# The second w2 block's remainder moved behind the last product group, and four terms of the first down tile moved into the second tile

## The chip, the cores and the metric

The kernel runs on one core of one Trainium2 chip. What is compared is the device time of one execution in microseconds (us). The kernel before took 725.92 us (median of 3 runs, 725.57 to 726.45). One more execution was taken with the hardware profiler on, and it is that one that all the rows below come from.

The engines are named as in the profile: PE is TensorE (matmul), PEld its weight load, DVE is VectorE, ACT is ScalarE, POOL is GpSimd, SP is SyncE, which issues most transfers.

## The reference

Attention with a decay over 8 batches and 8 heads, then a mixture of 8 experts that routes every one of the 4608 rows to one expert:

```python
def _moe_ref(x, w_gate, w1, w2):
    N, D, E, F = (4608, 512, 8, 1024)
    ...
    for e in range(E):
        mask = expert_idx == e
        ...
        xe = x[mask]
        h = np.maximum(xe @ w1[e], 0.0)
        ye = h @ w2[e]
        out[mask] = gate_w[mask, None] * ye
    return out.astype(np.float32)
```

All inputs and outputs are float32.

## The kernel before

The first half of the time is attention; the change does not touch it. From about 364 us on the kernel works through the experts 1 to 7 in one pattern, and every engine's instructions stand in an order that is written out by hand: the code runs through steps, and lists of tasks say which helper is called after which step.

**Two-part numbers.** A float32 product is made of three matmuls. Each operand is kept as a rounded part and a remainder (operand less rounded part), and a term is rounded times rounded, rounded times remainder, or remainder times rounded. For a weight block ACT makes the rounded part (a CAST) and DVE or POOL makes the remainder (a TENSOR_TENSOR subtraction, whose two inputs and whose output all lie in SBUF).

**Up phase of an expert** (`sevens`, L1515): h = relu(x @ w1), made by a scheme with seven products per group of columns, in four product groups 0 to 3, each of 7 x 6 matmuls: 168 in all, of 320, 288 or 256 columns depending on how many rows the expert has. After some of the products a step of `group` runs: ACT and DVE take the banks apart, and the last steps of a group (`end` and `last`: L1561 on ACT, L1592 and L1564 on DVE) write h as its rounded part `hh` and its remainder `hl`. For group 3 these last steps come after the last matmul of the phase, at the head of the down phase. DVE's steps there are, in order, L1581, L1582, L1583, L1564, L1592 and three more L1564.

**Down phase** (`down`, L1277): y = h @ w2 for five tiles m = 0 to 4 of 128 rows, each with 24 terms of 512 columns, 8 values of ft with 3 terms each. w2 comes in four blocks of two ft: block 1 is ft 2 and 3, block 3 is ft 6 and 7. `round_v(e, i)` is the CAST of block i on ACT (L1458), `rest_v(i)` its remainder on DVE (L1451), `split_v` is both. In the trace the remainders' tiles are called w_1w for all blocks; in the instruction order they are w2_0_1w (blocks 0 and 1) and w2_1_1w (blocks 2 and 3), while w2_0_0w and w2_1_0w are the rounded parts.

In tile 0 the values of ft come in the order 0, 1, 2, 4, 5, 6, 3, 7, since h of ft 3 and 7 is written last, and the terms that use block 3's remainder, (6, 0, 1) and (7, 0, 1), are put off: `finish_down` makes them after the first quarter (6 terms) of tile 1.

**The order around the change.** In the up phase the tasks hang on products 0 to 27. For experts 2 to 7, block 0 is split after product 10, block 2 after 16, block 1 after 23 (CAST and remainder), and block 3 gets its CAST after 24; its remainder is put off to the head of the down phase, behind the last steps of group 3:

```python
for i, k in enumerate((15, 22, 16) if e == 1 else (10, 23, 16)):
    at(ups, (k, S(self.split_v, i)))
at(ups, (23 if e == 1 else 24, S(self.round_v, 3)))
...
dns.setdefault(0, [])[:0] = [*self.ends, T(self.rest_v, 3)]
```

Behind that remainder DVE goes on with transposes of the next expert's rows (`flip`, L1180). POOL meanwhile works for the next expert: two sets of four additions (`sums_s`, L1398 to L1401, 128x256, all in SBUF), then two remainders of w1 (`rest_s`, L1419, 128x1024 and 128x768), which need a CAST of ACT (L1413) that stands behind the last L1561; then the scatters of finished rows (L1308). A tile's result leaves its bank through ACT (L1305); tiles 0, 2 and 4 use one bank, 1 and 3 another, and the next up phase's product 3 (T4) uses tile 4's bank.

## Time and profile before

| | us |
|---|---|
| median of 3 runs | 725.92 |
| the profiled execution's own time | 724.27 |
| its span, first to last instruction | 722.5 |
| PE busy in the span | 714.3 (99%) |
| DVE, ACT, POOL busy | 564.9, 498.6, 570.7 |
| mean granted TensorE clock | 0.994 |

The profiled execution is 1.65 us under the median, and 1.8 us of it lie outside the span. Rows of the timeline read: start in us from the span's start, duration in us, engine, line, operation, output tile <- input tiles, shapes, count of instructions put together, and in brackets the idle time of the engine before it with what ended it.

### The profile page before, as it was taken

The page shows a single profiled execution, that of the slowest core. Times are in us where ns is not written, and L with a number is a line of the kernel's source. Part 1 is how long each engine was busy: PE and PEld are TensorE (multiplying, and loading weights), DVE is VectorE, ACT ScalarE, POOL GpSimd, SP SyncE. Part 2 cuts the span into 40 slices and gives each one's busy share as a digit, 9 for nine tenths or more (in the row PEclk, how much of TensorE's full clock was granted, in tenths as well). Part 3 has the DMA queues.
Part 4 walks back from the last instruction along what each step waited for, and adds up shares of the span by engine and source line. Part 5 has one row for each costly group of instructions (what it writes and reads, how often), then busy time and mean ns, then how long its engine had stood idle before and what let it go on. Part 6 is the DMA issues. An engine that isn't in the chain of part 4 may idle for free. (4 is left out here: it accounts for less than half of the span.)

```text
span 722.5 us, 18439 instructions
## 1 busy us (share of the span) xinstructions
PE 714.3 (99%) x6321; PEld 617.4 (85%) x6321; DVE 564.9 (78%) x1610; ACT 498.6 (69%) x1319; POOL 570.7 (79%) x701
## 2 busy tenths in 40 slices
PE   9999999999999999999999999999999999999997
PEld 4788888888888888898999898898898898988985
DVE  6667888888888888771879859879589799897730
ACT  6999999999999999662646555566465575655631
POOL 6999989898989898884589779688788797997411
PEclk9999999999999999999999999999999999999999
DMA  7775787777777667244348376286475584673300
GB/s 197 197 195 165 195 215 192 212 191 209 204 203 197 216 193 231 81 165 129 111 163 271 118 233 206 96 265 195 149 220 165 175 240 136 217 216 116 119 30 35
DMA packets 98724, 127.59 MB, mean 177 GB/s; under 512 B 10287, under 2 KB 56367, under 8 KB 98608
## 3 DMA queue, kind: packets, MB, share of 16 engines
q1 hardware_dynamic: 91568, 106.12, 50.5%
q0 software_dynamic: 6400, 19.93, 8.6%
q8 instruction: 71, 1.16, 0.6%
q14 instruction: 45, 0.37, 0.2%
q10 hardware_dynamic: 640, 0.01, 0.0%
HBM read 99.12 MB, written 27.93 MB: 176 GB/s over the span
## 5 line engine op out<-in xcount | busy, mean ns | idle before, releaser
L422 ACT ACTIVATE sc<-sc,nmx 128x512 f32<-128x512 f32 (+3 forms) x256 | 142.3, 558 | 5.4 <-DVE nmx L379 4.3
L1515 PE MATMUL ps<-X_0w,w1s 128*128 128x320 f32 (+2 forms) x504 | 107.0, 303 | 0.2 <-DVE u L1574 0.2
L1277 PE MATMUL ps<-w_0w,hl 128*128 128x512 f32 x272 | 107.2, 394 | 0.0
L1277 PE MATMUL ps<-w_0w,hhw 128*128 128x512 f32 x273 | 106.3, 390 | 0.0
L1277 PE MATMUL ps<-w_1w,hhw 128*128 128x512 f32 x272 | 105.5, 392 | 0.0
L1308 POOL DMA_INDIRECT out<-y,si_fast x40 | 47.4, 1186 | 70.0 <-ACT y L1305 39.5
L467 ACT COPY aT<-ps 128x512 f32<-128x512 f32 (+1 forms) x224 | 93.4, 506 | 1.6 <-PE ps L455 0.5
L330 POOL TENSOR_TENSOR hl<-raw,hl 128x640 fp32r<-128x640 f32 (+1 forms) x60 | 89.6, 1494 | 5.0
L526 PE MATMUL ps<-aT,va_t 128*64 128x256 f32 (+3 forms) x896 | 91.2, 355 | 0.0
L1515 PEld LDWEIGHTS ps<-X_0w,w1s 128*128 128x128 f32 x504 | 82.3, 188 | 0.7 <-DVE u L1574 0.5
L526 PEld LDWEIGHTS ps<-aT,va_t 128*64 128x64 f32 x896 | 56.9, 138 | 28.9 <-issue 5.4
L403 PE MATMUL ps<-hl 64*128 64x512 f32 (+1 forms) x720 | 80.4, 340 | 0.0
L1515 PE MATMUL ps<-X_1w,w1s 128*128 128x320 f32 (+2 forms) x252 | 75.9, 301 | 0.0
L379 DVE CUSTOM_DVE_ANT_0 sc<-ps,bias 128x128 f32<-128x128 f32 (+1 forms) x128 | 59.8, 486 | 9.7 <-PE ps L403 4.6
L1305 ACT ACTIVATE y<-ps,g_fast 128x512 f32<-128x512 f32 x40 | 27.9, 698 | 56.5 <-PE ps L1277 52.6
L1419 POOL TENSOR_TENSOR w1s<-w1r,w1s 128x768 fp32r<-128x768 f32 (+1 forms) x32 | 62.7, 1968 | 0.1
L1277 PEld LDWEIGHTS ps<-w_0w,hhw 128*128 128x128 f32 x273 | 51.2, 188 | 11.4 <-ACT hhw L1561 0.3
L1277 PEld LDWEIGHTS ps<-w_1w,hhw 128*128 128x128 f32 x272 | 51.1, 188 | 11.6
L1277 PEld LDWEIGHTS ps<-w_0w,hl 128*128 128x128 f32 x272 | 51.1, 188 | 10.9 <-DVE hl L1564 0.5
L379 DVE CUSTOM_DVE_ANT_1 sc<-ps,bias 128x256 f32<-128x256 f32 (+1 forms) x128 | 57.7, 488 | 2.9 <-PE ps L403 2.8
L1515 PE MATMUL ps<-xa,w1s 128*128 128x320 f32 (+2 forms) x336 | 56.0, 302 | 0.3 <-PEq L1289 0.3
L403 PEld LDWEIGHTS ps<-hl 64*128 64x128 f32 x720 | 52.3, 185 | 3.3
(246 smaller groups left out, 1899.5 us busy)
## 6 DMA issues: line engine op xcount, KB each, us to landing
bias<-ud SPq DMA_DIRECT2D x30, 576.0 KB, 5.8
w1r<-in_w SPq DMA_DIRECT2D x112, 128.0 KB, 2.6
w<-in_w SPq DMA_DIRECT2D x28, 512.0 KB, 6.6
raw<-in_qkT SPq DMA_DIRECT2D x64, 160.0 KB, 3.5
raw<-in_qkT SPq DMA_DIRECT2D x64, 144.0 KB, 3.7
va_t<-in_va SPq DMA_DIRECT2D x32, 256.0 KB, 5.8
x_dram<-row SPq DMA_DIRECT2D x32, 256.0 KB, 2.3
xs<-xg SPq DMA_DIRECT2D x30, 256.0 KB, 3.5
```

Source lines behind the costliest of these rows:

```text
L330: return eng.tensor_tensor(hl[:, 1], raws[n][:, r : r + w], hl[:, 0].bitcast(F32), ALU.subtract)
L379: red_last[:] = [V.tensor_tensor_reduce(dst, src, in1, -0.125, init, ALU.add, ALU.min, nms[n][:, col : col + 1]).ins]
L403: note(nc.tensor.matmul(pb[j][:, o : o + w], q[js], k[js], start=(i == 0), stop=(i == len(terms) - 1),))
L422: A.activation(x, x, AF.Exp, bias=nms[n][:, 5 * j + t : 5 * j + t + 1], scale=-1.0, accum_out=ssums[b][:, t, 2 * p + j : 2 * p + j + 1])
L467: copy_on = {"a": lambda o, i: A.copy(o, i), "v": lambda o, i: V.tensor_copy(o, i)}
L526: note(nc.tensor.matmul(pv[j * HD : (j + 1) * HD, q0 - qa : qb - qa], l, r, start=(blk == 0), stop=(blk == nb - 1),))
L1277: c.note(nc.tensor.matmul(py, rows(hi_, ft), self.w2p[e, ft][wi], start=k == 0, stop=k == len(terms) - 1, skip_group_check=tail or head,))
L1305: nc.scalar.activation(y, py, AF.Copy, scale=g[:, s : s + 1])
L1308: nc.gpsimd.indirect_dma_start(out=self.out, out_offset=bass.IndirectOffsetOnAxis(ap=si[:, s : s + 1], axis=0), in_=y, in_offset=None, bou ...
L1419: (eng or self.nc.vector).tensor_tensor(lo, raw, hi.bitcast(F32), ALU.subtract)
L1515: self.nc.tensor.matmul(bank[:, 0:cols], w[:, wi, mat, kt], x[xi][:, kt, 0:cols], start=start and k == 0, stop=k == 5, skip_group_check=True,)
```

## The change

`rest_v(1)` is taken out of the up phase (where `split_v` did it after product 23, or 22 for expert 1) and put behind the last steps of group 3, ahead of `rest_v(3)`. ACT's CAST of block 1 stays where it was. In tile 0 the four terms that use the remainders of blocks 1 and 3, of ft 2, 6, 3 and 7, are put off instead of two; all four are made after the first quarter of tile 1.

```diff
         if head:
-            terms.sort(key=lambda t: t in ((6, 0, 1), (7, 0, 1)))
+            late = [(ft, 0, 1) for ft in (2, 3, 6, 7)]
+            terms.sort(key=lambda t: t in late)
...
-            some(3 * part[0], 3 * part[1] - (2 if head and part[1] == FT else 0))
+            n = len(terms) - len(late) if head else 3 * FT
+            some(min(3 * part[0], n), min(3 * part[1], n))
         if part[1] < FT:
             return
         if head:
-            self.finish_down = lambda: (some(len(terms) - 2, len(terms)), self.down_out(e, m, py, tail))
+            self.finish_down = lambda: (some(n, len(terms)), self.down_out(e, m, py, tail))
...
-                for i, k in enumerate((15, 22, 16) if e == 1 else (10, 23, 16)):
+                for i, k in ((0, 15), (2, 16)) if e == 1 else ((0, 10), (2, 16)):
                     at(ups, (k, S(self.split_v, i)))
-                at(ups, (23 if e == 1 else 24, S(self.round_v, 3)))
+                for i, k in ((1, 22), (3, 23)) if e == 1 else ((1, 23), (3, 24)):
+                    at(ups, (k, S(self.round_v, i)))
...
-                dns.setdefault(0, [])[:0] = [*self.ends, T(self.rest_v, 3)]
+                dns.setdefault(0, [])[:0] = [
+                    *self.ends, T(self.rest_v, 1), T(self.rest_v, 3)]
```

DVE at the change from up to down of expert 2, in the kernel before (hl_7579 and hhw_111 are the parts of h, u and ps are buffers of group 3):

```order
L1451 TENSOR_TENSOR w2_0_1w_95<-w2_0_1_94,w2_0_0w_93 128x1024
L1581 TENSOR_TENSOR u0_8958<-ps_8956,u0_8958 128x320
L1582 TENSOR_TENSOR pr_170<-u0_8958,pr_170 128x320
L1583 TENSOR_TENSOR u1_8959<-u0_8958,u1_8959 128x320
L1564 SCALAR_TENSOR_TENSOR hl_7579<-ps_8955,hhw_111 128x320
L1592 TENSOR_TENSOR ps_8957<-ps_8957,u2_9107 128x320
L1564 SCALAR_TENSOR_TENSOR hl_7579<-pr_170,hhw_111 128x320
L1564 SCALAR_TENSOR_TENSOR hl_7579<-u1_8959,hhw_111 128x320
L1564 SCALAR_TENSOR_TENSOR hl_7579<-ps_8957,hhw_111 128x320
L1451 TENSOR_TENSOR w2_1_1w_103<-w2_1_1_102,w2_1_0w_101 128x1024
L1180 STREAM_TRANSPOSE ps_9216<-xg_8759 128x4x4x32
```

The same place in the changed kernel, whose lines are numbered two higher there:

```order
L1583 TENSOR_TENSOR u0_8958<-ps_8956,u0_8958 128x320
L1584 TENSOR_TENSOR pr_170<-u0_8958,pr_170 128x320
L1585 TENSOR_TENSOR u1_8959<-u0_8958,u1_8959 128x320
L1566 SCALAR_TENSOR_TENSOR hl_7579<-ps_8955,hhw_111 128x320
L1594 TENSOR_TENSOR ps_8957<-ps_8957,u2_9107 128x320
L1566 SCALAR_TENSOR_TENSOR hl_7579<-pr_170,hhw_111 128x320
L1566 SCALAR_TENSOR_TENSOR hl_7579<-u1_8959,hhw_111 128x320
L1566 SCALAR_TENSOR_TENSOR hl_7579<-ps_8957,hhw_111 128x320
L1453 TENSOR_TENSOR w2_0_1w_95<-w2_0_1_94,w2_0_0w_93 128x1024
L1453 TENSOR_TENSOR w2_1_1w_103<-w2_1_1_102,w2_1_0w_101 128x1024
L1180 STREAM_TRANSPOSE ps_9216<-xg_8759 128x4x4x32
```

Block 1's remainder went from ahead of the last eight steps of h to behind them, so that the two remainders stand back to back, and both stand ahead of the transposes.

PE in expert 2 before, from the last four terms of tile 0's first part (bank ps_9184) over the first quarter of tile 1 (ps_9244) to the two terms put off, which the listing counts as one row:

```order
L1277 MATMUL ps_9184<-w2_0_1w_95,hhw_111 128x512
L1277 MATMUL ps_9184<-w2_0_0w_93,hl_7579 128x512
L1277 MATMUL ps_9184<-w2_1_0w_101,hhw_111 128x512
L1277 MATMUL ps_9184<-w2_1_0w_101,hl_7579 128x512
...
L1277 MATMUL ps_9244<-w2_0_0w_93,hl_7579 128x512
L1277 MATMUL ps_9184<-w2_1_1w_103,hhw_111 128x512 x2
L1277 MATMUL ps_9244<-w2_0_0w_93,hhw_111 128x512
```

And in the changed kernel, where tile 0 has the bank ps_9183 and tile 1 ps_9242:

```order
L1278 MATMUL ps_9183<-w2_0_0w_93,hl_7579 128x512
L1278 MATMUL ps_9183<-w2_1_0w_101,hhw_111 128x512
L1278 MATMUL ps_9183<-w2_1_0w_101,hl_7579 128x512
...
L1278 MATMUL ps_9242<-w2_0_0w_93,hl_7579 128x512
L1278 MATMUL ps_9183<-w2_0_1w_95,hhw_111 128x512
L1278 MATMUL ps_9183<-w2_1_1w_103,hhw_111 128x512
L1278 MATMUL ps_9183<-w2_0_1w_95,hhw_111 128x512
L1278 MATMUL ps_9183<-w2_1_1w_103,hhw_111 128x512
L1278 MATMUL ps_9242<-w2_0_0w_93,hhw_111 128x512
```

The terms with block 1's remainder left tile 0's first part, which has 20 terms now instead of 22, and the terms put off begin as the 27th matmul of the phase instead of the 29th, with block 3's remainder wanted by the 28th. The order of ACT's instructions is the same in both kernels, and POOL's and SP's differ only in where a few branch instructions stand between them.

## Rows read from the trace of the kernel before

**Rows 1.** Stages: down phases of experts 1, 2, 5, 6; columns as headed.
```profile
core 0: us, PE busy (x) PEld busy (x) DVE busy (x) ACT busy (x) POOL busy (x), PEclk, DMA share, GB/s
388.76:416.26 27.50, 27.50 (x122) 22.54 (x121) 23.83 (x50) 14.33 (x31) 22.08 (x19) 1.00 0.49 149
440.90:468.40 27.50, 27.50 (x122) 22.54 (x121) 26.38 (x50) 14.23 (x31) 20.25 (x17) 1.00 0.37 116
591.59:614.80 23.21, 22.87 (x99) 17.88 (x98) 22.09 (x49) 14.13 (x32) 18.77 (x15) 1.00 0.55 167
639.53:667.03 27.50, 27.50 (x122) 22.55 (x121) 24.02 (x49) 14.31 (x31) 22.67 (x20) 1.00 0.44 137
```

**Rows 2.** Timeline of PE, expert 5, the end of tile 0.
```profile
595.28 0.40 PE L1277 MATMUL ps<-w_0w,hl 128*128 128x512 f32 x1
...
596.32 0.50 PE L1277 MATMUL ps<-w_0w,hl 128*128 128x512 f32 x1
596.66 0.40 PE L1277 MATMUL ps<-w_0w,hhw 128*128 128x512 f32 x1
```

**Rows 3.** Timeline of DVE, expert 5, from up to down.
```profile
591.35 1.22 DVE L1451 TENSOR_TENSOR w_1w<-w,w_0w 128x1024 fp32r<-128x1024 f32 x1
592.49 0.48 DVE L1581 TENSOR_TENSOR u<-ps,u 128x320 f32<-128x320 f32 x1
...
595.79 0.48 DVE L1564 SCALAR_TENSOR_TENSOR hl<-ps,hhw 128x320 fp32r<-128x320 f32 x1
596.19 1.36 DVE L1451 TENSOR_TENSOR w_1w<-w,w_0w 128x1024 fp32r<-128x1024 f32 x1
```

**Rows 4.** Timeline of DVE, expert 2, from up to down.
```profile
438.99 1.52 DVE L1451 TENSOR_TENSOR w_1w<-w,w_0w 128x1024 fp32r<-128x1024 f32 x1 [0.57 <-ACT w_0w L1458]
...
444.25 1.36 DVE L1451 TENSOR_TENSOR w_1w<-w,w_0w 128x1024 fp32r<-128x1024 f32 x1
```

**Rows 5.** Timeline of POOL, expert 2, the same stretch.
```profile
439.39 1.72 POOL L1400 TENSOR_TENSOR w1r<-w1r 128x256 f32<-128x256 f32 x1
441.07 0.74 POOL L1401 TENSOR_TENSOR w1r<-w1r 128x256 f32<-128x256 f32 x1
...
444.49 1.72 POOL L1401 TENSOR_TENSOR w1r<-w1r 128x256 f32<-128x256 f32 x1
446.17 4.22 POOL L1419 TENSOR_TENSOR w1s<-w1r,w1s 128x1024 fp32r<-128x1024 f32 x2
```

**Rows 6.** Timeline of ACT, expert 2: the CASTs that POOL's L1419 needs.
```profile
443.35 1.77 ACT L1413 CAST w1s<-w1r 128x1024 fp32r<-128x1024 f32 x2
```

**Rows 7.** Timeline of PE, expert 2: the last matmul that L1581 waits for.
```profile
439.87 0.31 PE L1515 MATMUL ps<-X_1w,w1s 128*128 128x320 f32 x1
```

**Rows 8.** Timeline of DVE, expert 2, late in the down phase.
```profile
455.21 3.37 DVE L1419 TENSOR_TENSOR w1s<-w1r,w1s 128x1024 fp32r<-128x1024 f32 x1
...
462.04 4.78 DVE L1429 TENSOR_TENSOR X_1w<-X,X_0w 128x640 fp32r<-128x640 f32 x4
```

**Rows 9.** Timeline of POOL, expert 2, the same stretch.
```profile
455.61 1.88 POOL L1419 TENSOR_TENSOR w1s<-w1r,w1s 128x768 fp32r<-128x768 f32 x1
...
462.21 1.35 POOL L1398 TENSOR_TENSOR w1r<-w1r 128x256 f32<-128x256 f32 x1
463.64 1.21 POOL L1399 TENSOR_TENSOR w1r<-w1r 128x256 f32<-128x256 f32 x1
```

**Rows 10.** Timeline of DVE, expert 1: block 3's remainder.
```profile
392.38 1.36 DVE L1451 TENSOR_TENSOR w_1w<-w,w_0w 128x1024 fp32r<-128x1024 f32 x1
```

**Rows 11.** Timeline of DVE, expert 6: block 3's remainder.
```profile
642.72 1.36 DVE L1451 TENSOR_TENSOR w_1w<-w,w_0w 128x1024 fp32r<-128x1024 f32 x1
```

**Rows 12.** Timeline of ACT, expert 6: tile 4 of expert 5 leaves its bank.
```profile
616.60 0.69 ACT L1305 ACTIVATE y<-ps,g_fast 128x512 f32<-128x512 f32 x1
```

**Rows 13.** Timeline of PE, expert 6: product T4 begins in that bank.
```profile
617.53 0.46 PE L1515 MATMUL ps<-X_0w,w1s 128*128 128x320 f32 x2
```

**Rows 14.** Timeline of DVE, expert 5's up phase: its first step.
```profile
572.26 0.49 DVE L1574 TENSOR_TENSOR u<-ps,u 128x320 f32<-128x320 f32 x1 [1.53 <-PE ps L1515]
```

## Prediction

> **What bounds the kernel now.** I read the stages first, then PE's timeline at the borders of the stages, then DVE's and POOL's. In the full down phases PE is back to back: 120 matmuls in 27.50 us, 229 ns each [rows 1]. So a change that adds and removes no matmul can only act through moments in which PE stands. Of the stages shown only expert 5's has PE idle at all, 22.87 of 23.21 us [rows 1]; that expert has the fewest rows and so the shortest up phase, in which DVE falls behind. The moment that this change touches is the end of expert 5's tile 0. The 17th matmul of the down phase starts at 595.28. The 20th, at 596.32, should by the beat of 229 ns have come 0.35 us sooner, and the 21st follows it 0.34 us later instead of 0.23 [rows 2]. It waits for the last part of h, which DVE ended at 595.79 + 0.48 = 596.27 [rows 3]. Over the whole tile the delay is 0.46 us. The restart alone cost 0.1 us, and I use that below for every wait.
>
> **The change part by part.** No instruction is added or removed; two things move.
>
> *Block 1's remainder leaves the up phase.* In expert 5 it stood at 591.35 for 1.22 us directly ahead of L1581 at 592.49 [rows 3], whose own input was ready at about 591.1. All of the last eight DVE steps can come about 1.2 us sooner, and the tile wants h two matmuls (0.46 us) sooner than before because it has 20 terms ahead instead of 22. That is enough: the wait of 0.46 us goes. Elsewhere PE did not wait for h, so nothing is gained there; in expert 2, for one, the remainder held DVE until 438.99 + 1.52 = 440.51, and L1581's own last matmul ends at 439.87 + 0.31 = 440.18 [rows 4, 7], so h moves forward by some 0.25 us.
>
> *Both remainders now stand back to back behind h, and PE wants both sooner.* Block 1's is wanted by matmul 27 and block 3's by matmul 28, 27 x 229 ns = 6.19 us after the phase begins; before, block 3's was wanted by matmul 29, at 6.42 us. Between h and that moment DVE must fit two remainders. Alone each takes 1.2 us. But they are not alone: POOL works in SBUF at that time, and the rows show that the two do not run at once. A POOL addition takes 0.74 us by itself and 1.72 when a remainder of DVE falls on it (439.39 under the remainder of 438.99, 444.49 under that of 444.25) [rows 4, 5]; the remainder takes 1.36 or 1.52 then. When DVE has several such instructions in a row, POOL gets one of its own in between each time: four L1429 in 4.78 us, and a POOL addition ends inside each of them [rows 8, 9]. And when POOL's is a wide one, DVE stands for all of it: the DVE instruction of 455.21 took 3.37 us, ending 1.09 us after POOL's 1.88 us L1419 had ended at 457.49 [rows 8, 9].
>
> The rule behind it, in the Trainium skill's page SBUF — State Buffer, section "Who interferes with whom", is that a VectorE instruction with both inputs in SBUF and a GpSimd instruction that reads SBUF share one read port, held for a whole instruction by whichever came first while the other stands still. The rows above agree with it. By that rule a remainder pair is always open to a POOL instruction between the two, which gives the sum below; if the two merely slowed each other a little, by the 0.15 us of the 1.36 us rows, the sum would be that of the first rival.
>
> So the second remainder ends later than the first one's start by: first 1.2 to 1.3, one POOL instruction, second 1.2. With an addition in between (about 0.6 us in which it holds DVE off) that is 3.0 us. With POOL's 128x1024 L1419 in between it is 4.7: the two L1419 of rows 5 last 4.22, the 768-wide one 1.88 [rows 9], so the wide one 2.35 us. Which of them POOL has in hand decides each expert.
>
> Expert 2. POOL's L1419 began at 446.17 after being held up by two remainders, 0.98 us each (1.72 less 0.74) [rows 5]. Without the one of 438.99 and ahead of the other it would ask at about 444.2. It also needs the first CAST of 443.35, half of the pair and 1.05 us long, which moves forward with h, so it ends at about 444.15 [rows 6]. DVE's first remainder starts at 444.25 less the 0.25 gained and less some 0.15 of collisions that fall away: 443.85, ending at about 445.2. POOL has by then waited for a microsecond, so its wide L1419 goes next, until about 447.4, and block 3's remainder ends at 448.5. PE wants it at 440.90 + 6.19 = 447.09. PE stands **1.45 us**. Expert 4's phase repeats expert 2's to 0.02 us in all these rows: another **1.45**.
>
> Expert 1. POOL still has additions left, so one of these comes between. The first remainder stands where block 3's stood, 392.38 [rows 10] (POOL's later sums, held by a load, eat what DVE gains). End of the second: 395.4; wanted at 388.76 + 6.19 = 394.95 [rows 1]: **0.45**. Expert 5: 596.19 less 1.0 (1.2 less one more collision) = 595.2, plus 3.0 = 598.2, wanted at 591.59 + 6.19 = 597.78 [rows 1, 3]: **0.45**. Expert 6: 642.72 less 0.15 plus 3.0 = 645.6, wanted at 639.53 + 6.19 = 645.72 [rows 1, 11]: no wait, by 0.1 us. Expert 3 comes out the same way without a wait, and in expert 7 POOL has no such work left.
>
> *Queued behind the two remainders* are the transposes and all of DVE's work for the next expert. They come 2.9 us later in experts 2 and 4, of which PE's own delay takes off 1.55. The rest, 1.35 us, runs into the next up phase, where DVE's first step had 1.53 us of idle time before it [rows 14]: just covered. If that cover were gone, each further tenth would delay PE by about as much. ACT's exit of tile 2 and the scatters also move, with over 0.5 us left before their bank is wanted. In expert 5 DVE's work is late by 0.65 us while PE gains nothing net, and that shows at one place: expert 6's T4 starts at 617.53, only 0.24 us after ACT has emptied the bank at 616.60 + 0.69 [rows 12, 13], and that ACT step hangs on POOL and DVE. It costs between 0 and 0.5; I take 0.3.
>
> Sum: -0.46 + 1.45 + 1.45 + 0.45 + 0.45 + 4 restarts of 0.1 + 0.3 = **+4.0 us**. On the profiled execution 724.27 becomes 728.3, on the median 725.92 becomes 729.9. Bounds: only the two long waits with nothing else, -0.46 + 2.9 = +2.4 (728.3); with T4 at 0.5 and the wide L1419 in expert 6 too, which is missed by only 0.1 us, +1.6: +5.8 (731.7).
>
> **The rivals.**
>
> *DVE keeps its turn through both remainders.* Then the pair takes 2.6 us after the start, as two 1.36 us rows would: ending at 446.5 in expert 2 and at 597.8 in expert 5, against 447.09 and 597.78 wanted. No wait anywhere; 0.46 us is saved, of which T4 takes back what goes beyond its 0.24 us of slack: -0.2, 725.7. This is the side of "not slower". For it: where block 3's remainder stood it was held off by 0.16 us only (1.36 for 1.2) [rows 3, 4]. Against: the four L1429 in a row. It decides if DVE's second instruction is in line before POOL's is.
>
> *POOL's wide L1419 does not come between in experts 2 and 4*, because the CAST is later than I think or an addition is still due. Then these experts lose 446.85 - 447.09, nothing, and what stays is experts 1 and 5: -0.46 + 0.9 + 0.2 + 0.3 = about +0.9, 726.9.
>
> *The delay runs on.* DVE is busy for 26.38 of 27.50 us in expert 2's down phase [rows 1]; with more collisions in the shifted work the 1.53 us of rows 14 would not cover it, and the short up phase of expert 5 begins late on DVE. Each of two experts adds 0.5 to 1: +5.5, 731.4.
>
> *The change gains everywhere*: excluded beyond 0.46 us, since there is no other wait that it shortens.
>
> **How the numbers follow.** Forecast 0.65, DVE keeps its turn 0.17, no wide L1419 in between 0.09, runs on 0.08, anything else 0.01. About 0.2% (1.45 us) is what a measurement of this kernel can tell from no change. The forecast with nearly all of its bounds and the running on are slower by more than that; the first rival and two thirds of the second are within it. So slower 0.76, same 0.22, faster 0.02. The range leaves out the first rival and reaches from the second (with its 0.5 us of spread between runs) to the forecast's upper bound: 726.4 to 731.6.
>
> **What would show it.** Right: in experts 2 and 4 block 3's remainder lasts over 3 us, with POOL's 2.4 us L1419 inside it, and PE stands about 1.5 us at the 28th matmul of the phase; smaller waits there in experts 1 and 5; none at the end of expert 5's tile 0. Wrong: two remainders of 1.2 to 1.4 us in a row and a POOL instruction of twice its length, or an addition between them; or PE waiting at the 27th matmul, for block 1's, which would mean that POOL's L1419 came ahead of both.

## The result, and the profile after

The changed kernel takes 733.8 us (median; 729.47 to 734.63) against 725.75 for the kernel before beside it: ratio 1.0102, 95% interval 1.0082 to 1.0122, or 7.4 us more (5.9 to 8.9). The forecast was +4.0. It had the sign, the place and the mechanism of its two long waits right; the loss is about twice as large.

Line numbers of DVE, ACT, POOL and PE code are one or two higher after than before: L1278 for the down phase's matmuls (L1277), L1307 for y (L1305), L1310 for the scatter (L1308), L1421 for w1's remainder (L1419), L1453 for w2's (L1451), L1517 for the up phase's matmuls (L1515), L1576 for DVE's first step of a phase (L1574). The kernels of the experiments can be shifted by a few lines more.

First the answer on PE's waits from the start of expert 1 on. Columns: engine, output and line that waited, what it waited for; us in total, times, longest. The kernel before:

```profile
PE ps L1515 <- PEq L1289: 0.3, 1, 0.3
PE ps L1515 <- DVE u L1574: 0.2, 1, 0.2
```

The changed kernel:

```profile
PE ps L1278 <- DVE w_1w L1453: 3.3, 4, 1.3
PE ps L1278 <- issue: 1.2, 2, 0.6
PE ps L1517 <- PEq L1290: 0.8, 1, 0.8
PE ps L1517 <- ACT y L1307: 0.7, 1, 0.7
PE ps L1517 <- DVE u L1576: 0.5, 2, 0.3
```

The first row is the forecast: four waits for block 3's remainder. The other four rows are not in it. These rows count only idle time of PE and leave out short waits. So from here on a wait is the excess of the time from one matmul's start to the next over the beat of that stage (229 ns in a down phase), restart included. Between the first matmul of expert 1's up phase and the last matmul of the program there are 352.89 us before and 362.03 after, 9.14 more. It is made up so:

| place | before | after |
|---|---|---|
| matmul 28 of the down phase, block 3's remainder: experts 1, 2, 4, 5 | 0 | 0.56 + 1.60 + 1.61 + 0.64 = 4.40 |
| end of expert 5's tile 0 | 0.46 | 0 |
| inside tile 4, between its first and second matmul: experts 1, 2, 3, 4, 6 | 0 | 0.87 + 0.31 + 0.86 + 0.32 + 0.30 = 2.66 |
| the same branch in expert 5, which leads to expert 6 | 0.48 | 0.98 |
| expert 6's products T4 and T3 | 0 | 0.98 + 0.60 = 1.58 |

The rest of the 9.14, 0.46, is 0.14 in expert 1's up phase and parts of under 0.1 us in each other stage. Stages after, as in [rows 1]: experts 2 and 5, from the first matmul to that of the next stage.

```profile
443.72:473.16 29.44, 28.07 (x122) 22.39 (x121) 28.35 (x50) 14.22 (x31) 19.50 (x15) 1.00 0.37 110
599.24:623.17 23.93, 22.76 (x99) 17.91 (x98) 22.71 (x48) 12.43 (x30) 17.03 (x14) 1.00 0.55 171
```

Expert 2's down phase has grown from 27.50 to 29.44 us, and DVE's busy time with it, from 26.38 to 28.35. The granted clock is the full one in both.

**The forecast wait.** Timelines of DVE, POOL and PE in expert 2, which answer to [rows 4, 5]:

```profile
446.67 4.70 DVE L1453 TENSOR_TENSOR w_1w<-w,w_0w 128x1024 fp32r<-128x1024 f32 x2
...
447.00 6.08 POOL L1421 TENSOR_TENSOR w1s<-w1r,w1s 128x1024 fp32r<-128x1024 f32 x2
...
449.71 0.39 PE L1278 MATMUL ps<-w_1w,hhw 128*128 128x512 f32 x1
451.42 0.97 PE L1278 MATMUL ps<-w_1w,hhw 128*128 128x512 f32 x3 [1.33 <-DVE w_1w L1453]
```

The pair of remainders takes 4.70 us, just as forecast (4.7): 1.36 and 3.42 with a small overlap. POOL's wide one asked 0.33 us after the first began and went ahead of the second. Expert 4 repeats it; in experts 1 and 5 the pair takes 3.0 us with an addition in between.

**What was not forecast: tile 4.** Expert 1, timelines of DVE, ACT (its exit of tile 2) and POOL before:

```profile
403.36 1.21 DVE L1419 TENSOR_TENSOR w1s<-w1r,w1s 128x1024 fp32r<-128x1024 f32 x1
404.49 1.10 DVE L1180 STREAM_TRANSPOSE ps<-xg 128x512 f32<-128x512 f32 x1
...
406.20 0.72 ACT L1305 ACTIVATE y<-ps,g_fast 128x512 f32<-128x512 f32 x1
...
404.20 1.23 POOL L1308 DMA_INDIRECT out<-y,si_fast  x1 [3.81 <-DMA out<-y,si_fast]
405.44 1.87 POOL L1419 TENSOR_TENSOR w1s<-w1r,w1s 128x768 fp32r<-128x768 f32 x1
```

and after, with ACT's exit of tile 2 and PE:

```profile
406.35 3.43 DVE L1421 TENSOR_TENSOR w1s<-w1r,w1s 128x1024 fp32r<-128x1024 f32 x1
409.71 1.08 DVE L1180 STREAM_TRANSPOSE ps<-xg 128x512 f32<-128x512 f32 x1
...
405.82 1.00 POOL L1310 DMA_INDIRECT out<-y,si_fast  x1 [3.13 <-ACT w1s L1415]
406.82 1.87 POOL L1421 TENSOR_TENSOR w1s<-w1r,w1s 128x768 fp32r<-128x768 f32 x1
...
411.40 0.72 ACT L1307 ACTIVATE y<-ps,g_fast 128x512 f32<-128x512 f32 x1
...
412.68 0.39 PE L1278 MATMUL ps<-w_0w,hhw 128*128 128x512 f32 x1
413.68 0.50 PE L1278 MATMUL ps<-w_1w,hhw 128*128 128x512 f32 x1 [0.61 <-issue]
```

Before, DVE's 1024-wide remainder came while POOL was still idle and took 1.21 us. After, it comes 3 us later (1.7 us counted from the begin of the phase), while POOL is issuing a scatter; POOL's 768-wide remainder then goes first and DVE's takes 3.43. So it is in experts 3 and 5 too, and in 6 with 2.87; in experts 2 and 4 the two met in the kernel before already [rows 8, 9]. Behind it stands the transpose of tile 1, whose result ACT must copy before it can empty tile 2's bank (L1307, done at 411.40 + 0.72 = 412.12). Tile 4 is summed in that same bank. From phase begin to the end of that exit: 18.2, 20.0, 18.5, 20.2, 19.1, 17.7 us in experts 1 to 6 before, 22.0, 22.5, 21.4, 22.5, 21.9, 20.9 after.

The exit is still done before tile 4's first matmul (412.68). Yet PE waits, one matmul later. The view of the line that loads the two registers for the next expert tells why; columns: engine, operation, count; duration in ns min/median/max, first and last start. Before:

```profile
L1535 PEldq TENSOR_LOAD <-arms x1: 311/311/311, 407.0 to 407.0; - x1
L1535 PEldq TENSOR_LOAD <-tails x1: 297/297/297, 407.7 to 407.7; - x1
```

After:

```profile
L1537 PEldq TENSOR_LOAD <-arms x1: 307/307/307, 412.2 to 412.2; - x1
L1537 PEldq TENSOR_LOAD <-tails x1: 298/298/298, 412.9 to 412.9; - x1
```

The exit ends at 406.20 + 0.72 = 406.92 before. In both kernels the loads begin within 0.1 us of the exit's end: PE's sequencer, which runs ahead of the array, stops at tile 4's first weights until the bank is free, and only then reaches the loads and the branch behind them. From the exit's end to the second matmul that takes 413.68 - 412.12 = 1.56 us. Before, the exit came 3.9 us ahead of tile 4 (410.77) and the array was still busy with tile 3. After, it comes 0.6 us ahead, and 1.56 less 0.56 less 0.23 (the beat) is what is left to wait: 0.77, with a restart of 0.10.

**Expert 6's T4 and T3.** Timelines of ACT and PE, which answer to [rows 12, 13]:

```profile
625.10 1.05 ACT L1415 CAST w1s<-w1r 128x1024 fp32r<-128x1024 f32 x1 [0.40 <-POOL w1r L1401]
626.06 0.68 ACT L1307 ACTIVATE y<-ps,g_fast 128x512 f32<-128x512 f32 x1
...
626.79 0.57 PE L1517 MATMUL ps<-X_0w,w1s 128*128 128x320 f32 x2 [0.71 <-ACT y L1307]
...
629.16 0.56 PE L1517 MATMUL ps<-X_0w,w1s 128*128 128x320 f32 x2 [0.34 <-DVE u L1576]
```

The exit of tile 4 stands on ACT behind a CAST that waits for POOL's sums, as before, but 2.9 us into expert 6 instead of 1.8. T4 waits 0.98 instead of the 0.3 of the forecast, and T3, behind DVE's late first step, another 0.60.

### The profile page after: what moved, and what is told of

Read it like the earlier page. It is cut to its first block, busy times and chain, and to the rows that moved or that the text cites. A ratio compares the mean times of both kernels' runs of the same rounds, so it can differ in the third digit from the quotient of the medians.

```text
span 732.8 us, 18439 instructions
## 1 busy us (share of the span) xinstructions
PE 717.7 (98%) x6321; PEld 617.1 (84%) x6321; DVE 581.2 (79%) x1610; ACT 498.0 (68%) x1319; POOL 569.5 (78%) x701
## 4 chain that ended last, share of the span: by engine, by line
PE 82%; DVE 9%; POOL 4%; issue 2%; ACT 1%; DMA 1%; POOLq 0%; DVEq 0%; ACTq 0%
PE ps L1278 23%; PE ps L1517 16%; PE ps L526 12%; PE ps L403 10%; PE ps L455 8%; PE ps L437 4%; PE ps L450 3%; DVE w_1w L1453 2%; POOL w L1090 1%; PE pr L1517 1%; DVE w1s L1421 1%; PE ps L617 1%; PE ps L1229 1%; DVE hl L1566 1%; DVE X_1w L1431 1%
## 5 line engine op out<-in xcount | busy, mean ns | idle before, releaser
L1310 POOL DMA_INDIRECT out<-y,si_fast x40 | 45.3, 1131 | 82.8 <-ACT y L1307 63.9
L1278 PE MATMUL ps<-w_1w,hhw 128*128 128x512 f32 x272 | 104.9, 396 | 4.7 <-DVE w_1w L1453 3.3
L1517 PE MATMUL ps<-X_0w,w1s 128*128 128x320 f32 (+2 forms) x504 | 107.2, 303 | 1.3 <-ACT y L1307 0.7
L1278 PE MATMUL ps<-w_0w,hl 128*128 128x512 f32 x272 | 107.1, 394 | 0.0
L1278 PE MATMUL ps<-w_0w,hhw 128*128 128x512 f32 x273 | 106.5, 390 | 0.0
L1517 PEld LDWEIGHTS ps<-X_0w,w1s 128*128 128x128 f32 x504 | 82.3, 188 | 2.4 <-ACT y L1307 1.0
L1517 PE MATMUL ps<-X_1w,w1s 128*128 128x320 f32 (+2 forms) x252 | 75.9, 301 | 0.0
L1421 POOL TENSOR_TENSOR w1s<-w1r,w1s 128x768 fp32r<-128x768 f32 (+1 forms) x32 | 67.3, 2111 | 2.6 <-ACT w1s L1415 2.5
L1278 PEld LDWEIGHTS ps<-w_1w,hhw 128*128 128x128 f32 x272 | 50.7, 188 | 19.5 <-DVE w_1w L1453 5.0
L1278 PEld LDWEIGHTS ps<-w_0w,hhw 128*128 128x128 f32 x273 | 51.2, 188 | 11.2
L1307 ACT ACTIVATE y<-ps,g_fast 128x512 f32<-128x512 f32 x40 | 28.0, 699 | 47.6 <-PE ps L1278 42.7
L1278 PEld LDWEIGHTS ps<-w_0w,hl 128*128 128x128 f32 x272 | 51.1, 188 | 10.7
L1517 PE MATMUL ps<-xa,w1s 128*128 128x320 f32 (+2 forms) x336 | 56.0, 302 | 0.8 <-PEq L1290 0.8
```

The lines of the kernel that those rows point to most:

```text
L1278: c.note(nc.tensor.matmul(py, rows(hi_, ft), self.w2p[e, ft][wi], start=k == 0, stop=k == len(terms) - 1, skip_group_check=tail or head,))
L1310: nc.gpsimd.indirect_dma_start(out=self.out, out_offset=bass.IndirectOffsetOnAxis(ap=si[:, s : s + 1], axis=0), in_=y, in_offset=None, bou ...
L1421: (eng or self.nc.vector).tensor_tensor(lo, raw, hi.bitcast(F32), ALU.subtract)
L1517: self.nc.tensor.matmul(bank[:, 0:cols], w[:, wi, mat, kt], x[xi][:, kt, 0:cols], start=start and k == 0, stop=k == 5, skip_group_check=True,)
```

## The experiments

Theory A: the surplus over the forecast has causes of its own, tile 4's register loads, the collision of L1421, the CAST ahead of the exit, and each can be taken away. Theory B: all of it is one delay. DVE has so much to do in the down phase that 1.2 us more can't be caught up, and PE meets that delay at whichever hand-over comes first. Rivals to both: PE's new order is itself to blame, or the forecast wait is not what it seems.

The table gives the times against the kernel before (from the ratio, with its interval), the change of the 352.89 us, and the waits at three places. "Tile 4" counts expert 5's branch above its 0.48. The kernel before has 0.46 in expert 5's tile 0 and no other of these.

| kernel | time, us | stretch, us | block 3's remainder | tile 4 | expert 6's up phase |
|---|---|---|---|---|---|
| changed | +7.4 (5.9 to 8.9) | +9.14 | 4.40 | 3.16 | 1.58 |
| changed, once more | +9.0 (7.8 to 10.1) | +7.93 | 4.33 | 2.25 | 1.63 |
| 1 terms only | +0.7 (-0.6 to 2.0) | +0.60 | 0 | 0 | 0 |
| 2 six later | +7.5 (5.4 to 9.5) | +8.93 | 0.70 | 6.96 | 1.58 |
| 3 POOL's 768 later | +4.3 (2.8 to 5.9) | +5.97 | 4.47 | 0 | 1.94 |
| 4 loads early | +5.0 (3.3 to 6.7) | +6.18 | 4.16 | 0.05 | 2.21 |
| 5 wide pair later | +6.6 (5.2 to 8.0) | +6.39 | 1.29 | 3.57 | 1.59 |
| 6 before, DVE +1.2 | +2.8 (1.8 to 3.6) | +2.31 | 0 | 1.49 | 0.82 |
| 7 CAST behind y | +8.9 (7.8 to 10.0) | +6.42 | 4.07 | 2.47 | 0.15 |
| 8 before, h terms later | +0.2 (-0.6 to 1.0) | +0.56 | 1.11 | 0 | 0 |
| 9 three undone | +5.6 (4.6 to 6.7) | +4.61 | 2.49 | 0 | 1.96 |
| 10 all | +3.2 (2.2 to 4.3) | +3.64 | 0.40 | 0 | 2.54 |
| 11 h terms mended | +0.1 (-1.2 to 1.3) | 0.00 | 0 | 0 | 0.46 |
| 13 rest on POOL | +6.3 (4.3 to 8.3), less 1.86 | +4.05 | 4.23 | 0 | 0.35 |
| 14 the same, six later | +2.8 (1.7 to 3.9), less 1.84 | +0.84 | 0.39 | 0 | 0.87 |
| 15 before, rest on POOL | +2.1 (0.9 to 3.3), less 1.81 | +0.33 | 0 | 0 | 0.37 |
| 16 h terms, rest on POOL | +2.1 (0.9 to 3.3), less 2.16 | +0.43 | 0 | 0 | 0.91 |

"Less" is a stop of DVE's sequencer after the last tile in kernels 13 to 16, which has nothing to do with the question and is told at the end.

**1, terms only.** The remainder goes back to its old place; the four terms stay put off.

```diff
-                for i, k in ((0, 15), (2, 16)) if e == 1 else ((0, 10), (2, 16)):
+                for i, k in enumerate((15, 22, 16) if e == 1 else (10, 23, 16)):
...
-                    *self.ends, T(self.rest_v, 1), T(self.rest_v, 3)]
+                    *self.ends, T(self.rest_v, 3)]
```

> The four terms of tile 0 are still put off behind tile 1's first quarter, but block 1's remainder is back in the up phase, at its old place. Theory (the loss comes from the two remainders in one place on VectorE): no waits at the 28th matmul, none of the new ones in tile 4, and expert 5's 0.46 us at the end of tile 0 is gone, so 0.2 to 0.5 us faster than the kernel before. Rival (PE's own new order costs, since tile 0's bank is emptied later): slower than before by 1 us or more, with ScalarE's exits of tiles 0 and 2 later.

Every wait but those of expert 5 and 0.20 in expert 3 is gone, so PE's order is not to blame. My -0.46 was wrong: the wait at the end of expert 5's tile 0 doubles, to 0.93. Timelines of DVE and PE:

```profile
593.12 1.23 DVE L1453 TENSOR_TENSOR w_1w<-w,w_0w 128x1024 fp32r<-128x1024 f32 x1
...
598.10 0.50 PE L1278 MATMUL ps<-w_0w,hl 128*128 128x512 f32 x1 [0.26 <-DVE hl L1566]
```

With block 1's remainder still ahead of h on DVE, the put-off terms make PE want h two matmuls (0.46 us) sooner, and nothing pays for it. The prediction had both halves of this and I used only one.

**2, six later.** The four terms behind tile 1's second quarter: `(m, q) == (1, 1)` in place of `(1, 0)`.

> The changed kernel with the four terms made six matmuls (1.37 us) later, behind tile 1's second quarter. All theories: the waits for block 3's remainder (1.60, 1.61, 0.56, 0.64 us) fall to 0.1 to 0.3 in sum. Theory A (two separate losses): the tile 4 waits stay as they are, so the total is some 4 us below the changed kernel, +3.2 on the kernel before. Theory B (one delay of VectorE's chain, which PE meets first at the 28th matmul and again at tile 4): what PE no longer waits at the 28th matmul it waits at tile 4, in experts 2 and 4 about 1.9 instead of 0.3 us, and the total stays within 0.8 us of the changed kernel, about +7.

This tells A from B. The wait for block 3's remainder falls by 3.7 us, and tile 4's grows by 3.8. Timeline of PE in expert 2, where tile 4's wait was 0.31:

```profile
463.47 0.50 PE L1278 MATMUL ps<-w_0w,hhw 128*128 128x512 f32 x1
465.01 0.50 PE L1278 MATMUL ps<-w_1w,hhw 128*128 128x512 f32 x1 [1.04 <-issue]
```

PE comes sooner, ACT's exit does not; the time is the same. Between these two places it is B: one delay, met twice.

**3, POOL's 768-wide remainder later**, behind the scatter of tile 2 (slot 12 instead of 8).

> The changed kernel with GpSimd's 128x768 remainder of group 1 (L1421) moved behind the transpose of tile 1 and the scatter of tile 2, so that VectorE's 128x1024 remainder does not meet it. Theory (that collision delays ScalarE's exit of tile 2, and with it tile 4): VectorE's 1024-wide remainder takes 1.2 to 1.4 us instead of 2.9 to 3.4, the waits in tile 4 (3.15 us in sum with expert 5's) go, those at the 28th matmul (4.4) stay: +3.0 to +4.5 on the kernel before. Rival (the slip of the remainders alone makes the tile 4 waits, the collision is not needed): tile 4 still waits over 2 us in sum, +6 or more.

Timeline of DVE in expert 1:

```profile
403.82 1.22 DVE L1421 TENSOR_TENSOR w1s<-w1r,w1s 128x1024 fp32r<-128x1024 f32 x1
```

DVE's 1024-wide remainder takes 1.2 us in every expert, ACT's exit of tile 2 comes 1.7 to 2.2 us sooner, and tile 4 never waits. The theory's number holds in time, +4.3; the stretch is still 5.97 longer. T4 grows to 1.35, since POOL's sums now stand behind the 768-wide one.

**4, loads early.** The two register loads ahead of tile 4's first matmul.

```diff
-            some(0, 1)
             few = self.tail
             if e + 1 < E:
                 self.begin_up(e + 1)
-            else:
+            some(0, 1)
+            if e + 1 == E:
```

> The changed kernel with PE's two register loads for the next expert placed ahead of tile 4's first matmul instead of behind it. Theory (the wait inside tile 4 is the time of the register loads and the branch, which PE's sequencer can only begin once ScalarE has emptied the bank): with the loads done ahead, the gap between tile 4's first and second matmul falls below 0.3 us in every expert, expert 5's 1.2 us too: 3.2 to 3.9 us below the changed kernel, about +3.5 to +4.2 on the kernel before. Rival (the gap is a wait for data or the branch itself): the gaps stay, +7.4.

The exit of tile 2 is as late as in the changed kernel (0.8 us less so in expert 1, within 0.15 in the others), but the second matmul follows the first by 0.22 us. So the gap is the loads. Expert 1, the loads and PE:

```profile
L1537 PEldq TENSOR_LOAD <-arms x1: 308/308/308, 409.3 to 409.3; - x1
...
413.39 0.39 PE L1278 MATMUL ps<-w_0w,hhw 128*128 128x512 f32 x1
413.61 0.39 PE L1278 MATMUL ps<-w_1w,hhw 128*128 128x512 f32 x1
```

Two things differ from what I wrote. The branch in expert 5 still costs 0.53, as it did before the change, so that part is the taken branch and not the loads. And the stretch gains 2.96, not 3.2 or more, as expert 6 takes 0.6 of it back. So most of what is taken away at tile 4 is a gain here, although DVE is relieved of nothing: behind tile 4 the delay has slack up to expert 6. In this, and in 3, theory A holds.

**5, the wide pair later.** POOL's pair of remainders for the next expert in slot 4, behind the scatter of tile 0, instead of slot 2.

> The changed kernel with GpSimd's first pair of remainders for the next expert (128x1024 and 128x768, L1421) moved behind the scatter of tile 0, so that no wide instruction of GpSimd can come between VectorE's two w2 remainders. Theory (the wide one in between makes the 1.5 us of experts 2 and 4; an addition in between the 0.45 and 0.5 us of experts 1 and 5): block 3's remainder takes at most 1.8 us in every expert, the waits at the 28th matmul of experts 2 and 4 (3.2 us) go, those of experts 1 and 5 stay. Where the pair goes, it meets other work of VectorE; if it costs nothing there, +3 to +4 on the kernel before. If VectorE's delay is only moved (theory B of the run with six matmuls more), the waits in tile 4 grow instead and the total stays at +5.5 to +7.5.

The remainders of experts 2 and 4 take 1.36 and 1.21 us and their 1.6 us waits are gone; those of experts 1 and 5 stay. So the wide instruction in between is what made them, as the prediction said. In the stretch 2.75 us are gained, less than the 3.2 saved: expert 6's tile 4 now waits 0.81 instead of 0.30. In time, +6.6, it is hardly better than the changed kernel and lies where the expectation put a delay that is only moved, though tile 4 as a whole grew by only 0.4.

**6, the kernel before with 1.2 us more on DVE.** Group 1's 1024-wide remainder is done twice; nothing else.

> The kernel before with one more VectorE instruction: its 128x1024 remainder of group 1 (L1419) is done twice in experts 2 to 7's preparation. No w2 remainder and no term moves. Theory (tile 4 waits come from VectorE's chain alone, by way of the transpose of tile 1 and ScalarE's exit of tile 2): the second copy takes 1.2 us, or 2.9 to 3.4 where it meets GpSimd's 768-wide remainder; ScalarE's exit of tile 2 ends 1.2 to 3.4 us later than the 17.7 to 20.2 us of before, no wait appears at the 28th matmul, but waits of 0.2 to 2 us appear in tile 4, first of all in experts 2 and 4 with the least lead (2.0 and 1.9 us): +1.5 to +6 in all. Rival (the tile 4 waits need the w2 remainders or PE's order): within 0.5 us of the kernel before.

One instruction in each expert, far from any term that moved, costs 2.8 us. Timelines of DVE and PE in expert 2:

```profile
454.79 3.40 DVE L1426 TENSOR_TENSOR w1s<-w1r,w1s 128x1024 fp32r<-128x1024 f32 x1
458.23 1.22 DVE L1419 TENSOR_TENSOR w1s<-w1r,w1s 128x1024 fp32r<-128x1024 f32 x1
...
462.50 0.39 PE L1277 MATMUL ps<-w_0w,hhw 128*128 128x512 f32 x1
463.35 0.50 PE L1277 MATMUL ps<-w_1w,hhw 128*128 128x512 f32 x1 [0.46 <-issue]
```

ACT's exit of tile 2 comes 1.1 to 1.3 us later in every expert. Tile 4 waits in experts 2 and 4 and nowhere else, the two whose exit had the least lead in the kernel before; T4 and T3 of expert 6 wait again. These are waits at the places of the surplus without the change, 2.31 us of the changed kernel's 4.74 at these places.

**7, the CAST behind y.** Group 2's first rounding and remainder in slot 16 instead of 15, so that ACT empties tile 4's bank first.

> The changed kernel with the first rounding and remainder of group 2 (L1415, L1421 128x1024) moved behind tile 4, so that ScalarE empties tile 4's bank without first waiting for GpSimd's sums. Theory (expert 6's waits of 0.98 us at T4 come from ScalarE standing at that rounding ahead of the exit): the wait at T4 goes, and all others stay as they are; VectorE's first step of the next phase (L1576) now stands behind the remainder, which costs nothing where it has 1 us to spare, but expert 6's T3 wait of 0.6 us may grow: between -1.0 and +0.5 us on the changed kernel, +6.4 to +8 on the kernel before. Rival (the exit is late since tile 4 ends late): no change at T4.

T4's wait is gone in the trace. But in this execution DVE won its turn at the 1024-wide remainder of expert 5 (1.22 us), so the delay there was smaller anyway, and the time shows no gain. By itself it settles nothing; with kernel 9 it does.

**8 and 11, the kernel before with the last parts of h wanted later.** Both put the terms of ft 3 and 7 behind tile 1's first quarter; 8 has block 3's term of ft 6 first among them, 11 has block 3's two terms last.

```diff
-            terms.sort(key=lambda t: t in ((6, 0, 1), (7, 0, 1)))
+            low = [(6, 0, 1), (7, 0, 1)]
+            late = low + [t for t in terms if t[0] in (3, 7) and t not in low]
+            terms.sort(key=lambda t: (t in late) + (t in low))
...
```

> The kernel before, with all remainders at their old places; of tile 0 the six terms with the last two parts of h (ft 3 and 7) and block 3's term of ft 6 come behind tile 1's first quarter, so that PE wants the last of h six matmuls (1.37 us) later. Expected: expert 5's 0.46 us at the end of tile 0 goes, ScalarE's exit of tile 0 does not move, nothing else changes: -0.3 to -0.5 us on the kernel before. Rival (VectorE is late by more than this wait shows): a part of the wait comes back at tile 1, and the gain is under 0.2.

8 was badly built: its order wants block 3's remainder at the 24th matmul, and PE waits 0.85 for that in expert 5.

> The kernel before with the terms of the last two parts of h (ft 3 and 7) of tile 0 behind tile 1's first quarter, and block 3's two terms behind these, so that block 3's remainder is wanted no sooner than before. Expected: expert 5's 0.46 us at the end of tile 0 goes, no new wait: -0.3 to -0.5 us on the kernel before. Rival (the wait comes back at the put-off terms): no gain.

11 does what was meant: expert 5's tile 0 waits no more. The stretch is the same to 0.01 us. Timelines of ACT and PE at the start of expert 6:

```profile
616.09 1.05 ACT L1416 CAST w1s<-w1r 128x1024 fp32r<-128x1024 f32 x1 [1.23 <-POOL w1r L1402]
...
617.78 0.56 PE L1518 MATMUL ps<-X_0w,w1s 128*128 128x320 f32 x2 [0.20 <-ACT y L1308]
```

T4 waits 0.46, all that was gained. So the 0.46 us that the change was credited with were not to be had in this kernel.

**9, three undone.** 3, 4 and 7 together on the changed kernel.

> The changed kernel with three later waits taken away together: GpSimd's 768-wide remainder behind the scatter of tile 2, PE's register loads ahead of tile 4's first matmul, group 2's first rounding and remainder behind tile 4. Theory (what goes beyond the forecast is made of the tile 4 waits and expert 6's T4 and T3 alone): what stays is the forecast's own sum, the 28th matmul's waits in experts 1, 2, 4 and 5 (4.4 us) less expert 5's 0.46: +3.5 to +4.3 on the kernel before. Rival (the delay of VectorE finds PE at some further place): +5.5 or more, with new waits elsewhere.

The rival's time, +5.6; the trace has +4.61, with 2.49 at block 3's remainder instead of 4.40. Tile 4 and T4 are clear, and the delay is found at the next hand-over. Timelines of DVE and PE in expert 6:

```profile
621.53 1.75 DVE L1421 TENSOR_TENSOR w1s<-w1r,w1s 128x1024 fp32r<-128x1024 f32 x1
623.21 0.48 DVE L1576 TENSOR_TENSOR u<-ps,u 128x320 f32<-128x320 f32 x1
...
623.75 0.56 PE L1517 MATMUL ps<-X_0w,w1s 128*128 128x320 f32 x2 [1.50 <-DVE u L1576]
```

T3 waits 1.77 instead of T4's 0.98 and T3's 0.60, and expert 5's T3, which did not wait before, waits 0.5. (In expert 4 POOL had an addition in hand between the two remainders in this execution, and no wait followed; the same instructions in the same order can fall either way.)

**10, all.** 9, with the six matmuls of 2; the pair of 5 was meant to move too.

> The kernel of the run above, and in addition GpSimd's first pair of remainders behind the scatter of tile 0 and the four put-off terms six matmuls later. Theory: the waits at the 28th matmul go too (experts 2 and 4 by the pair, 1 and 5 by the six matmuls), and expert 5's 0.46 us stays gone: between -0.7 and +0.5 us on the kernel before. Rival (VectorE's 1.2 us more in the down phase must show on PE somewhere): +1.5 or more.

The rival again. With the put-off terms in the second quarter the scatter of tile 0 moved behind the pair, so the pair stood where it was, and the run shows 9 with 2 alone: no wait in tile 4, 0.40 at block 3's remainder, and 2.5 us at the start of expert 6, 1.75 of it at T3. For two more waits the table has no column: 0.3 us in expert 3's up phase and 0.9 in expert 5's, most of both at T3. So with the places in between cleared, the delay does reach the next up phase.

**12, the changed kernel once more**, for what varies.

> The changed kernel once more, unchanged. If VectorE and GpSimd meet by a hair in expert 5 (the remainder of group 1 took 3.2 us there, and 1.2 in one of its variants), this execution can differ there: the waits at the 28th matmul stay at 4.4 us in sum, those in tile 4 at 2.5 to 3.2 us, expert 6's T4 and T3 at 0 to 1.6 us. In time +6 to +8.5 us on the kernel before.

The 28th matmul's waits repeat to 0.1 us. In expert 1 DVE's remainder took 1.21 us this time, and tile 4 did not wait there; in expert 5 it took 3.40. Timelines of DVE and POOL in expert 1:

```profile
405.10 1.21 DVE L1421 TENSOR_TENSOR w1s<-w1r,w1s 128x1024 fp32r<-128x1024 f32 x1
...
405.00 0.99 POOL L1310 DMA_INDIRECT out<-y,si_fast  x1 [3.56 <-ACT w1s L1415]
```

The remainder began 0.10 us after the scatter, in the first execution 0.53 after it. So the meeting of DVE and POOL is decided by some tenths of a us, and two executions of one kernel differ by 0.87 us at this place.

**13 to 16, the 1024-wide remainder of group 1 on POOL**, which is idle for 3 us ahead of its own 768-wide one. This takes 1.2 us, or 3.4 with the collision, off DVE in each down phase.

```diff
-                       (7, N(self.split_s, 1, 0)), (8, N(self.round_s, 1, 1)),
-                       (8, N(self.rest_s, 1, 1, G)), (8, N(self.flip, 1)),
+                       (7, N(self.round_s, 1, 0)), (8, N(self.round_s, 1, 1)),
+                       (8, N(self.rest_s, 1, 0, G)), (8, N(self.rest_s, 1, 1, G)), (8, N(self.flip, 1)),
```

13 is the changed kernel with it:

> The changed kernel with the 128x1024 remainder of group 1 (L1421) on GpSimd instead of VectorE, directly ahead of GpSimd's 768-wide one; GpSimd stands idle for some 3 us ahead of it and 3.7 behind it. VectorE has 1.2 us less to do there, and 3.4 less where the two met. Theory (VectorE's amount of work in the down phase makes all that goes beyond the forecast): the tile 4 waits and expert 6's T4 and T3 waits go, those at the 28th matmul (4.4 us) stay: +3.3 to +4.5 on the kernel before. Rival (each wait has its own cause): tile 4 waits go, T4 and T3 stay at 1 us or more, +5 or more; or GpSimd, 2.4 us longer busy, becomes the late one.

Nearly all that goes beyond the forecast goes at once, in tile 4 and at T3; T4 keeps 0.35. What is left is the forecast: waits of 4.2 us for block 3's remainder and a stretch 4.05 us longer. PE's waits in it:

```profile
PE ps L1278 <- DVE w_1w L1453: 2.9, 3, 1.3
PE ps L1517 <- PEq L1290: 0.3, 1, 0.3
PE ps L1517 <- DVE u L1576: 0.2, 1, 0.2
```

The last two rows are those of the kernel before. 14 adds the six matmuls of 2:

> The kernel of e13 with the four terms six matmuls later. Theory: with VectorE relieved the waits at the 28th matmul fall to 0.3 us in sum and do not come back at tile 4 as they did when the terms alone were moved: between -0.7 and +1 us on the kernel before. Rival: they come back, +3 or more.

PE's waits in it:

```profile
PE ps L1517 <- ACT y L1307: 0.6, 1, 0.6
PE ps L1517 <- PEq L1290: 0.3, 1, 0.3
PE ps L1517 <- issue: 0.2, 1, 0.2
```

Now the waits at block 3's remainder go and do not come back in tile 4; 0.5 us of them comes back at T4. That makes +0.84 in the stretch, +0.95 in time without the end. The same edit that gained 0.2 us in 2 gains 3.2 here. That is B's strongest evidence. By themselves 13 and 14 do not tell DVE's amount of work from the collision of L1421, as they take away both. The six matmuls tell them apart, by one trace of each kernel: of the wait that they take away, 2 gains 0.21 of 3.70 us; 10, against 9, gains 0.97 of 2.09 with the collision gone and DVE's work as it was; 14, against 13, gains 3.21 of 3.84. So the collision is a part of the delay and the amount of work another. 15 and 16 put the remainder on POOL in the kernel before and in 11:

> The kernel before with the 128x1024 remainder of group 1 on GpSimd. The kernel before waits only for VectorE in expert 5 (0.46 us in tile 0, 0.5 us in the up phase), and neither lies behind that remainder: within 0.3 us of the kernel before. If GpSimd becomes late, slower by 0.5 us or more at expert 6's T4.

> The kernel of the run with the terms of h mended (expert 5's tile 0 wait gone, 0.46 us come back at expert 6's T4) with the 128x1024 remainder of group 1 on GpSimd. Theory (expert 6's T4 is VectorE's delay): the 0.46 us at T4 go too, -0.3 to -0.6 us on the kernel before. Rival (GpSimd's sums are what T4 waits for): T4 stays, within 0.2 us or slower.

15 is +0.33: nothing to win, as expected. In 16 the rival holds: T4 waits 0.91, more than without the move, as the CAST ahead of the exit waits for POOL's sums and POOL has 2.4 us more ahead of them. None of these kernels beats the one before.

## Why the prediction was right and wrong, point by point

- **Expert 5's tile 0, -0.46.** The wait went, by the path named (block 1's remainder out of h's way). It was no gain: kernel 11 takes away the same 0.46 alone and expert 6's T4 gives it all back. The prediction knew that T4 had 0.24 us of slack in the kernel before [rows 12, 13], and still booked the credit in full, with 0.3 for T4 beside it.
- **Experts 2 and 4, 1.45 each.** 1.49 and 1.50, with the restarts 1.60 and 1.61: right, with POOL's wide one in between, 3.42 us for block 3's remainder and the wait at the matmul named. Kernel 5 shows the cause. One reading behind it does not hold: that rows 8 and 9 agree with an order by first come. There DVE's remainder began 0.40 us ahead of POOL's wide one and ended 1.09 behind it, having begun while POOL was at a scatter; the same meeting makes L1421 late in the changed kernel.
- **Experts 1 and 5, 0.45 each.** 0.45 and 0.52 without the restart; experts 3, 6 and 7 do not wait, as said. That expert 1 comes out to the hundredth is luck in part: it is between 0.18 and 0.56 in kernels with the same code up to this place.
- **Restarts, 0.1 each.** 0.11.
- **T4, 0.3.** It waits 0.98, and T3 0.60: the term was mis-sized, as the wide remainder and the scatter of expert 5 moved too.
- **The step that failed**: "ACT's exit of tile 2 and the scatters also move, with over 0.5 us left before their bank is wanted." The lead was right, and even the half microsecond of it that would be left (0.6 to 1.1 us). But 0.5 is not enough: PE's sequencer still has the register loads and a branch to do after that exit, 1.56 us to the second matmul, so that hand-over needs some 1.3 us of lead. And in experts 1, 3, 5 and 6 the exit moved by 2.8 to 3.9 us, far more than the remainders alone moved DVE's work (1.7 us in expert 1), as the shifted L1421 ran into POOL's. That is 3.16 us which the sum had at nothing.
- **"Just covered" at the next up phase.** Right for the changed kernel: ahead of expert 5's first step DVE still has 1.17 us of idle time, where it had 1.53 [rows 14]. I had looked for the place where the delay would come out at the end of the chain; it came out in the middle.
- **The rivals.** That DVE keeps its turn, and that no wide one comes in between, did not happen in experts 2 and 4. That the delay runs on came nearest, at 0.08 and +5.5: its reason, more collisions in the shifted work, is what the trace shows; its place, expert 5's first step, is not. [Rows 1] held the warning: 26.38 of 27.50 us busy, with block 1's remainder added to it.

The two timings give +7.4 and +9.0, the two traces +9.14 and +7.93. Of the 1.21 us between the two traces 0.87 is tile 4 of expert 1, where the collision stayed away; why the times go the other way is open. How DVE and POOL share the blame for T4 stays open: 13 clears most of it, 16 does not.

## What to carry to other kernels

Here a move that added work to an engine which was 87 to 96% busy in the stage cost more than the first wait that showed: follow every hand-over of that engine down the stage, and ask for each what lead it needs, not just whether it is still ahead. A wait that is taken away at one hand-over is a gain only as far as the next one has slack; test that by moving the consumer later, and if the wait turns up again at the next place, relieve the producer instead. A wait of PE's sequencer for a bank also held back the register loads written behind it, so try them ahead of the wait.

## What the runs showed of the hardware

- From the end of ACT's exit, for which PE's sequencer waits, two register loads and a branch put the second matmul 1.55 to 1.61 us later (experts 1, 2, 3, 4 and 6 of the changed kernel). Nothing of it shows where the exit comes 1.85 us or more ahead of tile 4, as in the kernel before. With the loads ahead of the wait and the branch still behind it, the second matmul follows the first by 0.22 us (kernel 4).
- Where DVE's 1024-wide remainder of group 1 meets a scatter of POOL with POOL's 768-wide one behind it, the start decides. When it began 0.45 to 0.75 us after the scatter did, POOL's wide one went first and DVE's took 3.2 to 3.5 us, in 27 of 28 cases of all the traces (kernel 6's second copies left out); when it began up to 0.30 us after it, or up to 0.22 ahead of it, DVE's took 1.2, in 15 of 15. Between two such DVE instructions in a row a waiting TENSOR_TENSOR of POOL went first every time, as in [rows 8, 9].
- In kernels 13 to 16, with six DVE instructions fewer, the traced execution ends later by 1.81 to 2.16 us, behind the last tile and with no work in it. The view of the last branch's line in kernel 15:

```profile
L1763 DVEq COMPARE_BRANCH  x1: 72/72/72, 720.3 to 720.3; - x1
...
L1763 DVEq EVENT_SEMAPHORE  x1: 21/21/21, 724.0 to 724.0; - x1
```

  DVE's sequencer needs 3.7 us from its branch to the next instruction, where it needs 0.6 in the kernel before (719.5 to 720.1). The cause is open. It is taken out of the times above by the one trace of each kernel, as the stretch ends before it.
